# A token-mixer kernel whose phases are re-ordered as a software pipeline

## The chip, the cores and the metric

The kernel runs on one core of one Trainium2 chip. The metric is the time of one execution on the device, in microseconds (us). A profile's own length, its "span" from first to last instruction, is about 2 us shorter than that time. Engines: PE is the matmul array (TensorE), PEld its weight loads, DVE is VectorE, ACT is ScalarE, POOL is GpSimd, and SP issues most DMA transfers.

The kernel before scatters, and its slower runs have a lower granted array clock (0.903 at 284.3 us, 0.926 at 279.5 us). A run is called slow when it lies over 1.5% above the fastest.

## The reference

2048 tokens of width 448. A layer norm feeds two branches that are added at the end:

```python
x = A_x
xn = _layernorm(x, axis=-1)
return x + _A_ref(xn, A_wqkv, A_w_phi, A_wo) + _B_ref(xn, B_w1, B_w2, B_w3, B_w4)

# A: linear attention, 16 heads of 28
q, k, v = split(xn @ wqkv)
phi_q = concat(softmax(q @ w_phi), softmax(-(q @ w_phi)))    # phi_k from k alike
kv = einsum("bhsf,bhsd->bhfd", phi_k, v);  z = sum over s of phi_k
o  = (phi_q @ kv) / (phi_q @ z + 1e-6);    o @ wo

# B: mixer, then MLP
h  = gelu(layernorm(xn) @ w1)              # shifted by 1, -1, 2, -2 tokens in four channel groups
x1 = xn + shifted(h) @ w2
x1 + gelu(layernorm(x1) @ w3) @ w4         # w3 is 448x1792
```

## The kernel before

A small recorder notes each operation with what it reads and writes, then emits every engine's instructions in program order with the semaphore waits that the data needs. So the order of the Python calls is the order of each engine's queue. The work is cut into 16 tiles of 128 tokens, or 4 groups of 4 tiles. It has three stages:

```python
# front: layer norm, transposes of xn, W1
for g in range(NG):
    if g + 1 < NG:
        ln1(4 * g + 4, 4, [pool, dve])
    for i in range(4 * g, 4 * g + 4):
        xn_T(i)                       # PE transposes to banks 0, 1; ACT copies to xnT
    for m in range(NM):
        w1_chunk(g, m)                # PE; ACT applies gelu
        if g < 2:
            fold(1 - g, m)
# middle: K, V, W2 and Q of every tile, kv sums two tiles behind
for i in range(NT + 2):
    if i < NT:
        k_tile(i)
        v_tile(i)
    if i >= 2:
        kv_tile(i - 2)
    if i < NT:
        w2_tile(i)
        if i % 4 == 3:
            ln_scale(mv2, rs2, i - 3, 4)
        q_chunk(*divmod(i, 4))
kv_finish()
for i in range(4):
    g_apply(i)
    g_T(i, banks[7])
num_tile(0)
# tail: W3, W4, attention output; "fill" is dealt out between the 14 W3 chunks of a group
for g in range(NG):
    fill = []
    for j in range(4):
        i = 4 * g + j
        if i > 0:
            fill.append(lambda i=i: num_tile(i))
        if g + 1 < NG:
            fill.append(lambda i=i + 4: (g_apply(i), g_T(i, banks[7])))
        if i > 0:
            fill.append(lambda i=i - 1: o_T(i))
        if g >= 1:
            fill.append(lambda i=i - 4: fin_tile(i))
    ...                               # w3_chunk(g, fc), then the next entries of fill
```

Pieces of the tail (cut):

```python
def g_apply(i):                       # second layer norm of x1, on POOL
    ln_apply(pool, g_tok[:, i % 4, 0:D], xn[:, i, 0:D], rs2, i)
def g_T(i, b):                        # PE transposes g_tok into bank b; DVE copies to gT for W3
    ...
def num_tile(i):
    # PE: 8 matmuls of 128 columns to banks 5 and 6
    # DVE: reciprocal, three products and sums, sum, reciprocal (the "attention chain")
    R.ew(pool, "tensor_tensor", o_tok[...], q_n[...], rden[...], op=ALU.mult)   # POOL: output multiply
def o_T(i):                           # PE transposes o_tok into bank 7; DVE copies to oT
    ...
def fin_tile(i):                      # PE: 14 W4 and 4 wo matmuls of 448 columns; DVE adds; DMA out
    ...
```

Names in the profile are those of memory regions. In the tail the attention chain lives in the region `vaug`, h3T in `phik`, o_tok and oT in `hT` (in `xnT` after the change). `POOL hT<-vaug` is therefore the output multiply, and `bank<-ident,hT` the o transpose.

The softmax here doesn't subtract the row's maximum and nothing guards it: scores larger than these inputs give would overflow.

## Time and profile before

| | before |
|---|---|
| time, median of 4 runs | 279.68 us (277.62 to 284.34) |
| span of the profiled run | 282.5 us (it was a slow one, 284.2 us) |
| front, middle, tail | 0-43, 43-101.4, 101.4-282.5 us |

The first line of the profile page gives busy time, share of the span and instructions of each engine:

```profile
PE 223.5 (79%) x1277; PEld 123.7 (44%) x1289; DVE 121.2 (43%) x275; ACT 101.8 (36%) x184; POOL 93.6 (33%) x125
```

Two rows of its second part cut the span into 40 slices of 7 us; a digit is the PE's busy share, or the granted clock, in tenths:

```profile
PE   1587779999999946665866859587595959999996
...
PEclk9959999999999977989679786999977868999999
```

PE is the busiest engine, but neither row is full. The middle (slices 7 to 14) is dense at full clock. From slice 15 both rows dip again and again. The busy time in four stretches says the same in numbers; after the stretch come its length, the busy time (and instructions) of PE, PEld, DVE, ACT and POOL, the granted clock, DMA share and GB/s:

```profile
0.00:42.97 42.97, 27.80 (x194) 18.44 (x195) 18.39 (x48) 27.01 (x45) 18.28 (x48) 0.92 0.60 175
42.97:101.40 58.43, 56.66 (x321) 33.07 (x319) 43.81 (x81) 41.36 (x83) 32.12 (x28) 1.00 0.00 1
101.40:237.00 135.60, 96.49 (x514) 49.71 (x524) 43.34 (x109) 25.08 (x42) 31.43 (x38) 0.82 0.02 7
237.00:282.50 45.50, 42.51 (x252) 22.47 (x252) 15.63 (x38) 8.36 (x14) 11.81 (x12) 1.00 0.07 23
```

The long stretch from 101.4 us is the weak one: clock 0.82, and 39 us without a matmul. The waits view tells for what PE waited (total us, times, longest):

```profile
PE bank L190 <- POOL g_tok L198: 35.9, 13, 3.3
PE bank L190 <- DMA hi<-in_A_wqkv_dram: 5.7, 1, 5.7
PE bank L190 <- DVE xn L198: 2.9, 1, 2.9
```

One of the 13 waits, in the timeline (start, duration, engine, line, operation, and in brackets the idle time before it and what ended it):

```profile
130.42 1.52 DVE L198 TENSOR_TENSOR vaug<-bank,vaug 128x16 f32<-128x16 f32 x3
...
132.53 0.94 POOL L198 TENSOR_TENSOR hT<-vaug 128x448 bf16<-128x448 f32 x1 [6.15 <-DVE vaug L198]
133.45 0.72 POOL L198 TENSOR_SCALAR g_tok<-xn,rs 128x448 bf16<-128x448 bf16 x1
134.22 0.60 PE L190 MATMUL bank<-ident,g_tok 128*128 128x128 bf16 x4 [3.27 <-POOL g_tok L198]
...
134.62 1.91 PE L186 MATMUL bank<-gT,w 128*128 128x512 bf16 x4
```

POOL was idle for 6.15 us, and g_apply needs nothing that was late: it reads x1 and its statistics, ready since the middle. But it stands behind the output multiply in POOL's queue, and that waits for the attention chain on DVE. PE, which has the g transpose next, waits 3.27 us for a 0.72 us operation that could have run long before. The four 512-column matmuls after the hole take 1.91 us, at a granted clock of 0.50. The four at 126.67 us took 1.03 us, at a clock of 1.00. These two durations are what "half rate" and "full rate" mean below.

### The profile page before, as it was taken

To read this page: it belongs to the slowest core of one execution; us is meant where nothing else is said; L and a number is where in the kernel's file an instruction comes from. 1 tells how busy PE (TensorE), PEld (TensorE's weight loads), DVE (VectorE), ACT (ScalarE), POOL (GpSimd) and SP (SyncE) were. 2 spreads that over 40 slices of the span, in tenths; PEclk is the share of its full clock that TensorE was granted. 3 is DMA by queue.
4 is the path that set the end of the run, shared out by engine and by line. 5 is a ranking of instruction groups with operands and counts; after the bars stand their busy time and mean duration, and the time that the engine had idled before them with its cause. 6 is when DMAs were issued, how large, how long until landed. Compare 5 with 4: busy or idle time off the path is not lost.

```text
span 282.5 us, 3255 instructions
## 1 busy us (share of the span) xinstructions
PE 223.5 (79%) x1277; PEld 123.7 (44%) x1289; DVE 121.2 (43%) x275; ACT 101.8 (36%) x184; POOL 93.6 (33%) x125
## 2 busy tenths in 40 slices
PE   1587779999999946665866859587595959999996
PEld 0554445555555623332433424233252424555552
DVE  5377204877777754433313140441413131434311
ACT  1668768666666631323211011121111111232100
POOL 8544402464646482222031230303303030222520
PEclk9959999999999977989679786999977868999999
DMA  7997000000000000000000000000000000000000
GB/s 212 331 310 210 1 1 2 0 0 2 0 0 2 0 0 0 2 0 0 0 0 19 1 16 0 16 19 0 16 1 18 2 16 16 18 17 16 19 32 32
DMA packets 9613, 9.52 MB, mean 34 GB/s; under 512 B 1022, under 2 KB 9150, under 8 KB 9598
## 3 DMA queue, kind: packets, MB, share of 16 engines
q1 hardware_dynamic: 8176, 8.09, 9.7%
q10 hardware_dynamic: 1422, 1.23, 1.4%
q8 instruction: 10, 0.16, 0.2%
q14 instruction: 5, 0.04, 0.0%
HBM read 7.48 MB, written 1.84 MB: 33 GB/s over the span
## 4 chain that ended last, share of the span: by engine, by line
PE 67%; DVE 15%; POOL 12%; ACT 3%; issue 2%; POOLq 0%
PE bank L186 62%; DVE vaug L198 10%; PE bank L190 5%; POOL hT L198 4%; POOL g_tok L198 3%; DVE st L198 2%; ACT xnT L194 2%; POOL rs L198 1%; DVE xn L198 1%; POOL vaug L198 1%; ACT phik L194 1%; POOL kvq L198 1%; DVE mv L198 1%; POOL phik L198 1%; DVE gT L198 0%
## 5 line engine op out<-in xcount | busy, mean ns | idle before, releaser
L194 ACT ACTIVATE phik<-bank 128x512 bf16<-128x512 f32 (+1 forms) x88 | 49.2, 581 | 128.5 <-PE bank L186 128.5
L186 PE MATMUL bank<-gT,w 128*128 128x512 bf16 x212 | 63.2, 429 | 1.3 <-issue 0.4
L198 DVE TENSOR_TENSOR vaug<-bank,vaug 128x464 f32<-128x464 f32 (+2 forms) x64 | 33.3, 520 | 57.9 <-PE bank L186 56.3
L198 POOL TENSOR_TENSOR hT<-vaug 128x448 bf16<-128x448 f32 x16 | 15.1, 941 | 124.3 <-DVE vaug L198 124.3
L186 PE MATMUL bank<-w,phik 128*128 128x448 bf16 x224 | 50.3, 381 | 0.0
L198 POOL TENSOR_TENSOR phik<-phik,rks 128x896 bf16<-128x896 bf16 x16 | 27.2, 1698 | 36.0 <-DVE rks L198 35.8
L190 PE MATMUL bank<-ident,g_tok 128*128 128x128 bf16 x64 | 8.2, 270 | 37.6 <-POOL g_tok L198 35.9
L186 PEld LDWEIGHTS bank<-w,phik 128*128 128x128 bf16 x224 | 23.5, 106 | 24.3 <-issue 7.3
L186 PEld LDWEIGHTS bank<-gT,w 128*128 128x128 bf16 x224 | 22.8, 109 | 20.5 <-issue 6.9
L198 DVE TENSOR_REDUCE ksum<-phik 128x32 f32<-128x896 bf16 x16 | 17.3, 1082 | 23.3 <-ACT phik L194 23.3
L190 PEld LDWEIGHTS bank<-ident,g_tok 128*128 128x128 bf16 x64 | 4.7, 116 | 44.5 <-POOL g_tok L198 42.0
L186 PE MATMUL bank<-xnT,w 128*112 128x512 bf16 x64 | 17.6, 417 | 2.8 <-ACT xnT L194 2.8
L198 DVE COPY gT<-bank 128x512 bf16<-128x512 bf16 x16 | 6.8, 424 | 29.7 <-PE bank L190 29.7
L198 POOL TENSOR_TENSOR vaug<-xn,xtok 128x448 f32<-128x448 bf16 x16 | 16.5, 1032 | 5.7 <-DVE vaug L198 5.7
L194 ACT ACTIVATE hi<-bank 112x512 bf16<-112x512 f32 (+1 forms) x20 | 12.4, 681 | 11.6 <-PE bank L186 9.1
L186 PE MATMUL bank<-xnT,wpq 128*112 128x512 bf16 x64 | 16.5, 379 | 0.0
L186 PE MATMUL bank<-w,hT 112*128 112x448 bf16 x64 | 14.8, 352 | 0.0
L186 PE MATMUL bank<-wo,hT 128*128 128x448 bf16 x64 | 14.7, 353 | 0.0
L186 PE MATMUL bank<-wv,xnT 128*128 128x448 bf16 x64 | 14.7, 352 | 0.0
L186 PE MATMUL bank<-wpk,xnT 128*128 128x448 bf16 x64 | 14.7, 352 | 0.0
L198 DVE COPY hT<-bank 128x512 bf16<-128x512 bf16 x16 | 6.5, 408 | 13.8 <-PE bank L190 13.8
L194 ACT ACTIVATE hT<-bank 112x512 bf16<-112x512 f32 x16 | 9.6, 598 | 7.4 <-PE bank L186 7.2
(68 smaller groups left out, 250.6 us busy)
## 6 DMA issues: line engine op xcount, KB each, us to landing
out_dram<-vaug SPq DMA_DIRECT2D x16, 112.0 KB, 1.7
w<-in_B_w_dram SPq DMA_DIRECT2D x1, 1568.0 KB, 15.0
xtok<-in_A_x_dram SPq DMA_DIRECT2D x3, 448.0 KB, 8.0
w<-in_B_w_dram SPq DMA_DIRECT2D x1, 1344.0 KB, 10.8
hi<-in_A_wqkv_dram ACTq DMA_DIRECT2D x1, 672.0 KB, 4.7
xtok<-in_A_x_dram SPq DMA_DIRECT2D x4, 112.0 KB, 5.0
w<-in_B_w_dram SPq DMA_DIRECT2D x1, 392.0 KB, 9.3
w<-in_B_w_dram ACTq DMA_DIRECT2D x1, 336.0 KB, 7.4
```

What stands on the lines that cost most here:

```text
L186: self.op("PE", lambda e: e.matmul(out, lhsT, rhs, start=start, stop=stop, skip_group_check=True), [out], [lhsT, rhs])
L190: self.op("PE", lambda e: e.transpose(out, in_, ident), [out], [in_, ident])
L194: self.op("ACT", lambda e: e.activation(out, in_, func, **kw), [out], [in_] + aps)
L198: self.op(eng, lambda e: getattr(e, name)(out, *args, **kw), [out], aps)
```

## The change

The intent was a software pipeline: x is loaded first; V and W2 tiles are spread over the stages to even out the load; transposes run behind their inputs; the end of the kv sum is worked into the W3 stage. Matmuls and their shapes stay. The diff, cut to its core:

```diff
+        load_x(0, 2)
+        load_x(2, 2)
+        load_rows(wqk, A_wqkv[:, 0:896])        # was first, on ACT's queue
 ...
-            R.act(vaug[:, i, :]..., b[:, 0:D]..., ACT.Copy)
+            R.ew(dve, "tensor_copy", vaug[:, i, :]..., b[:, 0:D]...)
 ...
         for g in range(NG):                      # front
             ...
+            for i in range(4 * g + 4, min(4 * g + 8, NT)):
+                xn_T(i)                          # of the next group
+            if g < 2:
+                for i in range(4 * g, 4 * g + 4):
+                    v_tile(i)                    # 8 of the 16 V tiles
 ...
         for i in range(NT + 2):                  # middle
             if i < NT:
                 k_tile(i)
-                v_tile(i)
 ...
-                w2_tile(i)
-                if i % 4 == 3:
-                    ln_scale(mv2, rs2, i - 3, 4)
+                if i % 2 == 0:
+                    v_tile(8 + i // 2)
+                else:
+                    w2_tile(i // 2)              # W2 tiles 0 to 7
+                    ...
                 q_chunk(*divmod(i, 4))
+                if i == 9:
+                    for j in range(4):
+                        g_apply(j)
+                if i >= 12:
+                    g_T(i - 12, banks[5])
 ...
         for g in range(NG):                      # tail
             fill = []
+            if g + 1 < NG:
+                fill.append(lambda g=g: [g_apply(4 * g + 4 + j) for j in range(4)])
+            if g == 0:
+                fill.append(kv_blocks)
             for j in range(4):
                 i = 4 * g + j
-                if i > 0:
-                    fill.append(lambda i=i: num_tile(i))
+                fill.append(lambda i=i: num_tile(i))
+                if g >= 1:
+                    fill.append(lambda i=i - 4: fin_tile(i))
+                if g < 2:
+                    fill.append(lambda i=i + 8: w2_tile(i))     # W2 tiles 8 to 15
+                    ...
                 if g + 1 < NG:
-                    fill.append(lambda i=i + 4: (g_apply(i), g_T(i, banks[7])))
+                    fill.append(lambda i=i + 4: g_T(i, banks[7]))
                 if i > 0:
                     fill.append(lambda i=i - 1: o_T(i))
-                if g >= 1:
-                    fill.append(lambda i=i - 4: fin_tile(i))
```

More of the change, by code (lines that the diff above doesn't have):

```diff
@@ L244, in bass_parallel_sum__linear_kernel_hedgehog__mixer_s_mlp__prompt_kernel @@
         xn = new("xn", NT * 512).rearrange("p (t d) -> p t d", t=NT)
-        xnT = new("xnT", KC * S).rearrange("p (c s) -> p c s", c=KC)
+        xnT_r = region("xnT", KC * S * 2)
+        xnT = view(xnT_r, KC * S).rearrange("p (c s) -> p c s", c=KC)
         hT_r = region("hT", NM * HW * 2)
@@ L286, in bass_parallel_sum__linear_kernel_hedgehog__mixer_s_mlp__prompt_kernel @@
         h3T = view(phik_r, 2 * FC * 512).rearrange("p (b c f) -> p b c f", b=2, c=FC)
-        oT = view(hT_r, 2 * KC * 512).rearrange("p (b c s) -> p b c s", b=2, c=KC)
-        o_tok = view(hT_r, 4 * 512, at=2 * KC * 512 * 2).rearrange("p (b d) -> p b d", b=4)
+        oT = view(xnT_r, 2 * KC * 512).rearrange("p (b c s) -> p b c s", b=2, c=KC)
+        o_tok = view(xnT_r, 4 * 512, at=2 * KC * 512 * 2).rearrange("p (b d) -> p b d", b=4)
         o2 = 0
@@ L318, in bass_parallel_sum__linear_kernel_hedgehog__mixer_s_mlp__prompt_kernel, with load_x, load_rows @@
         dve, pool = "DVE", "POOL"
-        for i in range(4):
-            R.dma(xtok[:, i, :], x2d[128 * i:128 * i + 128, :])
-        def load_rows(dst, src, eng):
-            R.dma(dst[:, 0:3, :], src[0:384, :].rearrange("(c p) d -> p c d", p=128), eng)
-            R.dma(dst[0:64, 3, :], src[384:448, :], eng)
-        R.act(maskb[0:1, 0:1], ident[0:1, 0:1], ACT.Gelu_apprx_tanh) if False else None
-        load_rows(wqk, A_wqkv[:, 0:896], "ACT")
-        R.dma(wphi[0:DH, :].rearrange("e (h f) -> e h f", h=H), A_w_phi.rearrange("h e f -> e h f"), "ACT")
-        load_rows(w1, B_w1, "ACT")
-        for g in range(1, NG):
-            R.dma(xtok[:, 4 * g:4 * g + 4, :], x2d[512 * g:512 * g + 512, :].rearrange("(j p) d -> p j d", p=128))
-        load_rows(wv, A_wqkv[:, 896:1344], "SP")
+        def load_x(i, n):
+            R.dma(xtok[:, i:i + n, :], x2d[128 * i:128 * (i + n), :].rearrange("(j p) d -> p j d", p=128))
+        def load_rows(dst, src):
+            R.dma(dst[:, 0:3, :], src[0:384, :].rearrange("(c p) d -> p c d", p=128))
+            R.dma(dst[0:64, 3, :], src[384:448, :])
+        R.dma(wphi[0:DH, :].rearrange("e (h f) -> e h f", h=H), A_w_phi.rearrange("h e f -> e h f"), "ACT")
+        load_x(0, 2)
+        load_x(2, 2)
+        load_rows(wqk, A_wqkv[:, 0:896])
+        load_rows(w1, B_w1)
+        load_x(4, 4)
+        load_x(8, 4)
+        load_rows(wv, A_wqkv[:, 896:1344])
+        load_x(12, 4)
         R.dma(w2[0:CR, :, :], B_w2.rearrange("(m p) d -> p m d", p=CR))
-        load_rows(wo, A_wo, "SP")
-        load_rows(w3, B_w3, "SP")
+        load_rows(w3, B_w3)
+        load_rows(wo, A_wo)
         R.dma(w4[:, :, :], B_w4.rearrange("(c p) d -> p c d", p=128))
@@ L384, in ln_apply, with ln1_stats @@
             R.ew(eng, "tensor_scalar", dst, src, rst[:, i, 1:2], rst[:, i, 0:1], op0=ALU.add, op1=ALU.mult)
-        def ln1(a, n, engs):
+        def ln1_stats(a, n):
             for i in range(a, a + n):
@@ L389, in ln1, with ln1_apply @@
             ln_scale(mv, rs, a, n)
+        def ln1_apply(a, n, engs):
             for i in range(a, a + n):
@@ L429, in w1_chunk @@
             R.act(hT[0:CR, m, 2 + 512 * g:2 + 512 * g + 512], b[0:CR, :], ACT.Gelu_apprx_tanh)
+        rot = [(0, 1, 2, 3, 4, 5)]
         def rot_b():
-            return bank(0, 1, 2, 3, 4, 5)
+            return bank(*rot[0])
         def v_tile(i):
@@ L437, in v_tile @@
                 R.mm(b[:, 0:D], xnT[:, kc, 128 * i:128 * i + 128], wv[:, kc, :], kc == 0, kc == KC - 1)
-            R.act(vaug[:, i, :].rearrange("p (h e) -> p h e", e=HP)[:, :, 0:DH],
-                  b[:, 0:D].rearrange("p (h e) -> p h e", e=DH), ACT.Copy)
+            R.ew(dve, "tensor_copy", vaug[:, i, :].rearrange("p (h e) -> p h e", e=HP)[:, :, 0:DH],
+                 b[:, 0:D].rearrange("p (h e) -> p h e", e=DH))
         def k_tile(i):
@@ L457, in kv_tile, with kv_copy @@
                      i == 0 and c % 2 == 0, i == NT - 1)
-        def kv_finish():
+        def kv_copy():
             for h in range(2):
@@ L462, in kv_finish, with kv_blocks @@
                      banks[6 + h][:, 0:448].rearrange("p (c f) -> p c f", c=2))
+        def kv_blocks():
             b = banks[6]
@@ L542, in fin_tile @@
             R.dma(out2d[128 * i:128 * i + 128, :], outb[:, i % 4, :])
-        ln1(0, 2, [dve])
-        ln1(2, 2, [dve])
-        for t in range(2):
+        ln1_stats(0, 2)
+        ln1_stats(2, 2)
+        ln1_apply(0, 2, [dve])
+        ln1_apply(2, 2, [dve])
+        for t in (1, 0):
             for pair in range(2):
@@ L550, in bass_parallel_sum__linear_kernel_hedgehog__mixer_s_mlp__prompt_kernel @@
         phi_blocks()
+        for i in range(4):
+            xn_T(i)
+        ln1_stats(4, 4)
+        ln1_stats(8, 4)
+        ln1_apply(4, 4, [pool, dve])
+        rot[0] = (5, 6, 7)
         for g in range(NG):
-            if g + 1 < NG:
-                ln1(4 * g + 4, 4, [pool, dve])
-            for i in range(4 * g, 4 * g + 4):
-                xn_T(i)
             for m in range(NM):
@@ L559, in bass_parallel_sum__linear_kernel_hedgehog__mixer_s_mlp__prompt_kernel @@
                     fold(1 - g, m)
+            if g == 0:
+                ln1_stats(12, 4)
+                ln1_apply(8, 4, [pool, dve])
+            if g == 1:
+                ln1_apply(12, 4, [pool, dve])
+            for i in range(4 * g + 4, min(4 * g + 8, NT)):
+                xn_T(i)
+            if g < 2:
+                for i in range(4 * g, 4 * g + 4):
+                    v_tile(i)
+        rot[0] = (0, 1, 2, 3, 4, 5)
         for i in range(NT + 2):
@@ L566, in bass_parallel_sum__linear_kernel_hedgehog__mixer_s_mlp__prompt_kernel @@
             if i < NT:
-                w2_tile(i)
-                if i % 4 == 3:
-                    ln_scale(mv2, rs2, i - 3, 4)
-                q_chunk(*divmod(i, 4))
-        kv_finish()
+                if i % 2 == 0:
+                    v_tile(8 + i // 2)
+                else:
+                    w2_tile(i // 2)
+                    if i % 8 == 7:
+                        ln_scale(mv2, rs2, i // 2 - 3, 4)
+                q_chunk(*divmod(i, 4))
+                if i == 9:
[3 more added lines that the diff above has]
+                    g_T(i - 12, banks[5])
+                    rot[0] = (0, 1, 2, 3, 4)
+        kv_copy()
         R.ew(pool, "memset", o_tok[:, :, D:512], 0.0)
-        for i in range(4):
-            g_apply(i)
-            g_T(i, banks[7])
-        num_tile(0)
+        rot[0] = (3, 4)
         for g in range(NG):
             fill = []
+            if g + 1 < NG:
+                fill.append(lambda g=g: [g_apply(4 * g + 4 + j) for j in range(4)])
+            if g == 0:
+                fill.append(kv_blocks)
             for j in range(4):
                 i = 4 * g + j
-                if i > 0:
-                    fill.append(lambda i=i: num_tile(i))
+                fill.append(lambda i=i: num_tile(i))
[3 more added lines that the diff above has]
+                    fill.append(lambda i=i + 8: w2_tile(i))
+                    if j == 3:
+                        fill.append(lambda i=4 * g + 8: ln_scale(mv2, rs2, i, 4))
                 if g + 1 < NG:
-                    fill.append(lambda i=i + 4: (g_apply(i), g_T(i, banks[7])))
+                    fill.append(lambda i=i + 4: g_T(i, banks[7]))
                 if i > 0:
                     fill.append(lambda i=i - 1: o_T(i))
-                if g >= 1:
-                    fill.append(lambda i=i - 4: fin_tile(i))
             n = 0
```

## The prediction

> **What bounds it now.** TensorE (busy 79% of the span; the chain of waits is 62% matmul), but it runs well in only one of three stages. From busy time and granted clock by stretch:
>
> - Front (0-43 us: norms, transposes, W1): matmul busy 27.8 us. By the timeline each group of four tiles loses 1.05 us (transposes have two banks, emptied by 0.6 us ACT copies) plus 0.7 us before W1; the first W1 matmuls run at half rate.
> - Middle (43-101.4): no gaps, clock 1.00, 3.5 us per tile; 1.5 us wait for POOL at its end.
> - Tail (101.4-282.5): the waits view gives 35.9 us in 13 waits (up to 3.3 us) of the g transposes for POOL's g_tok. Each g_apply stands in POOL's queue behind the output multiply (0.94 us), which waits for the DVE attention chain (2.3 us). After such holes the clock falls: four 512-column matmuls start over 1.71 us instead of 0.86; mean clock 0.82 in 101.4-237. The last group, without g transposes (237-264), runs dense at 1.00.
>
> [...] after the 3.27 us gap before 134.2 the clock is 0.50, while the front's ~1 us gaps leave 1.00.
>
> **Work.** Matmul counts stay. From trace rates (0.215 us per 512 columns, 0.19 per 448, about 0.056 per 128) all matmul work is about 195 us at full clock (estimate). So about 85 us of 279 is holes and slow clock, some 60 of it in the tail.
>
> **What the change does.**
> 1. Four g_applys go to the head of each group's POOL work, a group early: the 35.9 us of waits and the half-rate stretches after them go. Main effect.
> 2. Eight V tiles (6.1 us of PE) fill the front's holes; eight W2 tiles (6.1 us) move to the tail.
> 3. V copies (0.57 us) move from ACT to DVE. Middle per two tiles: PE 5.5 us, DVE about 4.9 plus overheads, ACT 4.6. Nearly balanced: small stalls.
>
> **New stages (estimates from trace durations).**
> - Front: wqk queues behind x, so PE starts about 1 us later, but POOL's rs (8.6 us) and ACT's wT copies gate W1 anyway. Two-bank waits stay. End about 42, with 8 V tiles done.
> - Middle: 16x2.76 + 0.9 = 45 us of PE. The chain k matmul, exp, reduce, reciprocal, POOL, kv takes 4.7 us against 5.5 available; four g_applys at tile 9 (2.9 us of POOL) and ln_scale (1.4 us) overrun that; the last kv waits about 2 us. About 50 us.
> - Tail: first group DVE-bound: per tile 2.3 chain + 1.4 W2 add and statistics + 0.83 copies = 4.5 us, against 4.8 PE, and the o transpose shares bank 7 with the g transpose, whose copy queues behind the statistics: 1-2 us stall per tile, about 24 us. Groups 2-4 about 35, 31, 29; last four outputs 14; end 3. About 135.
>
> Sum: **227 us, 80% range 216 to 240**. Chances: faster by over 2% 0.98, within 0.015, slower 0.005.
>
> **What would show each step.** PE wait for g_tok below 3 us; tail clock at least 0.97; PE busy falls from 223 to 200-208; middle waits for POOL phik, largest near tile 9 and at the end; tail waits of transposes for the copy of gT, mostly in the first two groups; front about 42 us; ACT busy down 9 us, DVE up 9.
>
> **What would make it wrong.** If 1-2 us stalls in the first tail group trip the clock: 235-245. If DVE delays the kv chain every tile: +5-10. If the front's V tiles wait for DVE copies behind the norm statistics: +3. If bank-7 stalls are mostly hidden: 217.

A rule for idle gaps that no trace or run of this case shows is cut from the prediction, with the remark that the trace agrees with it; the measured gaps stay. Its sum: 42 + 50 + 135 = 227 us.

## The result

| | before | after |
|---|---|---|
| time, median of 4 runs | 279.68 us | 233.80 us (233.19 to 234.70) |
| ratio, 95% interval | | 0.838 (0.832 to 0.844) |
| span of the profiled run | 282.5 us | 231.3 us |
| front / middle / tail | 43.0 / 58.4 / 181.1 us | 46.5 / 48.8 / 136.0 us |

Ratios are the mean time of one kernel's fast runs over that of the kernel before in the same rounds, so not quite the ratio of the medians. The stages do not hold the same work: before, the tail is counted from the end of the kv sum, 7 us ahead of the first W3 matmul (108.4 us); after, it starts with the first W3 matmul (95.3 us), and eight W2 tiles have moved into it.

The same views of the changed kernel. Busy times:

```profile
PE 204.6 (88%) x1289; PEld 115.9 (50%) x1289; DVE 128.1 (55%) x291; ACT 94.8 (41%) x168; POOL 93.1 (40%) x125
```

The 40 slices, now of 5.8 us:

```profile
PE   0568989798999999696999889989999999999995
...
PEclk9988999999999999998899999999999999999999
```

The stretches:

```profile
0.00:46.46 46.46, 32.51 (x225) 20.89 (x226) 22.03 (x56) 26.99 (x45) 17.97 (x48) 0.96 0.59 162
46.46:95.29 48.83, 45.60 (x273) 27.61 (x272) 37.83 (x68) 34.39 (x67) 31.52 (x25) 1.00 0.00 1
95.29:231.30 136.01, 126.52 (x794) 67.39 (x792) 68.20 (x167) 33.43 (x56) 43.61 (x53) 0.98 0.04 14
```

The waits of PE:

```profile
PE bank L190 <- DMA hi<-in_A_wqkv_dram: 8.3, 2, 8.2
PE bank L190 <- DVE gT L198: 5.6, 6, 2.1
PE bank L186 <- POOL phik L198: 3.2, 3, 1.7
PE bank L190 <- ACT xnT L194: 2.9, 3, 1.1
PE bank L186 <- ACT xnT L194: 1.5, 2, 0.8
```

The 35.9 us of waits for g_tok are gone, and the clock of the tail is 0.98. PE's busy time fell by 19 us although it does the same matmuls: far fewer of them run at half rate (the W3 matmuls of 512 columns take 386 ns each on average instead of 429). The front, however, became 3.5 us longer, with 8 V tiles more in it (6.1 us of PE). Its PE timeline shows how few of them went into holes. The first W1 matmuls and the step from the x transposes to W1 of group 1, before:

```profile
15.70 1.95 PE L186 MATMUL bank<-xnT,w 128*112 128x512 bf16 x4 [0.75 <-ACT xnT L194]
...
23.90 0.87 PE L190 MATMUL bank<-ident,xn 128*128 128x128 bf16 x8 [1.05 <-POOL rs L198]
25.46 1.07 PE L186 MATMUL bank<-xnT,w 128*112 128x512 bf16 x4 [0.69 <-ACT xnT L194]
```

and after:

```profile
15.63 1.95 PE L186 MATMUL bank<-xnT,w 128*112 128x512 bf16 x4 [0.69 <-ACT xnT L194]
...
23.21 0.87 PE L190 MATMUL bank<-ident,xn 128*128 128x128 bf16 x8 [1.05 <-POOL rs L198]
23.92 3.19 PE L186 MATMUL bank<-wv,xnT 128*128 128x448 bf16 x16
26.95 1.03 PE L186 MATMUL bank<-xnT,w 128*112 128x512 bf16 x4
```

W1 starts at the same time, though PE's first instruction comes 2.5 us later (8.18 against 5.65 us). In group 1 the step takes 3.74 us instead of 1.56, so of 3.03 us of V tiles only 0.85 went into a hole. Group 2 is alike (0.93). That makes 1.8 of 6.1 us; another 0.6 us came from the W1 chunks of group 0, which happened to run at half rate for a shorter time (the second and third took 1.64 and 1.03 us instead of 1.91 and 1.24).

A new wait is the one for the copy of gT. The longest, in the timeline of the first tail group:

```profile
96.77 2.80 POOL L198 TENSOR_SCALAR g_tok<-xn,rs 128x448 bf16<-128x448 bf16 x4
...
104.96 0.39 PE L190 MATMUL bank<-ident,g_tok 128*128 128x128 bf16 x4
...
105.63 0.56 DVE L198 TENSOR_TENSOR xn<-bank,xn 128x448 bf16<-128x448 f32 x1
...
106.23 0.63 DVE L198 BATCH_NORM_STATS2 st<-xn 128x6 f32<-128x448 bf16 x1
106.89 0.18 DVE L198 BATCH_NORM_AGGREGATE mv<-st 128x2 f32<-128x6 f32 x1
106.99 0.39 DVE L198 COPY gT<-bank 128x512 bf16<-128x512 bf16 x1
...
107.44 0.40 PE L190 MATMUL bank<-ident,xnT 128*128 128x128 bf16 x4 [2.09 <-DVE gT L198]
...
107.67 1.85 PE L186 MATMUL bank<-gT,w 128*128 128x512 bf16 x4
```

The four g_applys (first line) are done at 99.57 us, 5.4 us before the transpose at 104.96. The o transpose at 107.44 uses the same bank 7, which is free only when DVE has copied gT out, and that copy stands behind the W2 add and statistics. After this hole of 2.09 us four 512-column matmuls took 1.85 us at a clock of 0.52: half rate once more.

### The profile page after: what moved, and what is told of

It reads as the page before. It is cut to its first block, busy times and chain, and to the rows that moved or that the text cites. A ratio compares the mean times of both kernels' runs of the same rounds, so it can differ in the third digit from the quotient of the medians.

```text
span 231.3 us, 3260 instructions
## 1 busy us (share of the span) xinstructions
PE 204.6 (88%) x1289; PEld 115.9 (50%) x1289; DVE 128.1 (55%) x291; ACT 94.8 (41%) x168; POOL 93.1 (40%) x125
## 4 chain that ended last, share of the span: by engine, by line
PE 62%; DVE 20%; POOL 7%; ACT 5%; DMA 3%; issue 2%; SPq 1%; DVEq 0%
PE bank L186 57%; DVE vaug L198 8%; PE bank L190 5%; DVE st L198 5%; POOL phik L198 3%; DMA hi<-in_A_wqkv_dram 3%; DVE xn L198 2%; DVE mv L198 1%; DVE ksum L198 1%; DVE gT L198 1%; POOL vaug L198 1%; POOL xnT L198 1%; POOL g_tok L198 1%; ACT phik L194 1%; ACT hi L194 1%
## 5 line engine op out<-in xcount | busy, mean ns | idle before, releaser
L186 PE MATMUL bank<-gT,w 128*128 128x512 bf16 x224 | 57.8, 386 | 0.0
L186 PE MATMUL bank<-w,phik 128*128 128x448 bf16 x224 | 45.0, 352 | 0.0
L198 POOL TENSOR_TENSOR xnT<-vaug 128x448 bf16<-128x448 f32 x16 | 15.1, 941 | 73.8 <-DVE vaug L198 73.8
L186 PEld LDWEIGHTS bank<-w,phik 128*128 128x128 bf16 x224 | 21.8, 98 | 20.7
L186 PEld LDWEIGHTS bank<-gT,w 128*128 128x128 bf16 x224 | 20.8, 99 | 18.3 <-issue 1.1
L186 PE MATMUL bank<-wo,xnT 128*128 128x448 bf16 x64 | 14.7, 352 | 0.0
L198 DVE CAST vaug<-bank 128x448 bf16<-128x448 f32 x16 | 9.5, 593 | 8.6 <-PE bank L186 7.8
L198 DVE RECIPROCAL vaug<-bank 128x16 f32<-128x16 f32 x16 | 4.1, 257 | 15.2 <-PE bank L186 15.2
L190 PE MATMUL bank<-ident,xnT 128*128 128x128 bf16 x64 | 6.3, 221 | 6.3 <-DVE gT L198 5.6
L186 PE MATMUL bank<-phik,vaug 128*128 128x224 bf16 x64 | 8.8, 259 | 3.2 <-POOL phik L198 3.2
```

Source lines behind the costliest of these rows:

```text
L186: self.op("PE", lambda e: e.matmul(out, lhsT, rhs, start=start, stop=stop, skip_group_check=True), [out], [lhsT, rhs])
L190: self.op("PE", lambda e: e.transpose(out, in_, ident), [out], [in_, ident])
L198: self.op(eng, lambda e: getattr(e, name)(out, *args, **kw), [out], aps)
```

## The experiments

Twelve kernels ran, all gave the right result, and all their runs were fast but one of e6 (229.6 us, left out of its ratio). "Before" is that kernel on the same chip, in the same job. By the record's own classing e8, e2, e6, e5 and e12 are "faster" than it and the others "unclear"; but all intervals end at 0.963 or below.

| run | what it is | us | before | ratio (95%) |
|---|---|---|---|---|
| e1_hoist_only | before + hoist | 240.8 | 281.5 | 0.858 (0.852-0.864) |
| e7_fin_first | before + lag | 246.0 | 281.5 | 0.876 (0.870-0.882) |
| e8_both | before + hoist + lag | 234.2 | 280.4 | 0.838 (0.833-0.843) |
| e3_warm_holes | before + dummy matmuls in the holes | 267.6 | 281.5 | 0.954 (0.945-0.963) |
| e2_unhoist | after - hoist | 245.1 | 280.4 | 0.875 (0.869-0.882) |
| e4_no_spread | after - spread of V and W2 | 231.0 | 281.5 | 0.822 (0.816-0.828) |
| e6_gT_first | after, g transpose ahead of W2 | 228.7 | 280.4 | 0.815 (0.808-0.823) |
| e5_wqk_first | after, wqk loaded first | 232.4 | 280.4 | 0.833 (0.826-0.839) |
| e9_early_rs | e4 + wqk first + POOL memsets later | 228.3 | 280.0 | 0.821 (0.811-0.830) |
| e10_best | e9 + front re-ordered | 230.5 | 280.0 | 0.828 (0.818-0.838) |
| e11_warm_start | e10 + dummy matmuls at the start | 229.4 | 280.0 | 0.824 (0.817-0.832) |
| e12_combined | e9 + selected parts of e10 | 226.6 | 279.8 | 0.815 (0.809-0.820) |

The theory: the gain is the waits for g_tok and the half-rate matmuls behind them, and two small moves in the tail's order take them away. The rival: the spread of V and W2, the loads and the late kv finish carry a good part.

### One part alone: the hoist

```diff
             fill = []
+            if g + 1 < NG:
+                fill.append(lambda g=g: [g_apply(4 * g + 4 + j) for j in range(4)])
 ...
-                    fill.append(lambda i=i + 4: (g_apply(i), g_T(i, banks[7])))
+                    fill.append(lambda i=i + 4: g_T(i, banks[7]))
```

> The kernel before with one part of the change: the four g_apply calls of the next group stand at the head of each group's POOL work. Theory A (the gain is the 35.9 us of waits for g_tok plus the half-rate matmuls after them; the rest of the re-ordering adds little): PE waits for g_tok below 3 us from 107 us on, mean clock of the tail 0.97 or more, time 231 to 240 us. Theory B (the moved V and W2 tiles, the x-first loads and the late kv finish each carry a part): 245 us or more.

Measured 240.8 us, just above theory A's range and well below theory B's. The clock from its first W3 matmul on (108.8 us) is 0.99. Its waits of PE:

```profile
PE bank L190 <- DVE gT L198: 10.1, 12, 1.6
...
PE bank L190 <- POOL g_tok L198: 0.9, 2, 0.5
```

The waits for g_tok went from 35.9 to 0.9 us. But 10.1 us of a wait appeared that had been 1.7 us: with the g transposes no longer late, the o transpose now follows while the gT copy is still queued on DVE. Three lines of order are worth 40.7 us.

### The other part alone: the lag

```diff
                     fill.append(lambda i=i: num_tile(i))
+                if g >= 1:
+                    fill.append(lambda i=i - 4: fin_tile(i))
                 if g + 1 < NG:
                     fill.append(lambda i=i + 4: (g_apply(i), g_T(i, banks[7])))
 ...
-                if g >= 1:
-                    fill.append(lambda i=i - 4: fin_tile(i))
```

> The kernel before with another part alone: in each slot the output tile of the group before is put ahead of the g transpose, so that 3.4 us of matmuls cover the POOL chain; g_apply stays where it was. There is no such tile in group 0. If the lag alone is enough where it exists: waits for g_tok fall from 35.9 to about 13 us (4 times 3.3 in group 0), time about 243 us (237 to 250). If only the place in POOL's queue counts: 270 us or more.

Measured 246.0 us, as expected. Its waits for g_tok:

```profile
PE bank L190 <- POOL g_tok L198: 9.8, 5, 3.3
```

The four over 1 us are in group 0 (1.19 to 3.27 us). Where an output tile stands between, its 3.4 us of matmuls cover the chain through DVE and POOL.

### Both, and nothing else

> The kernel before with the two parts of the earlier runs together: g_apply at the head of the group, and the output tile ahead of the g transpose. Alone they gave 240.8 and 246.0 us from 281.5. Theory A (both remove the same waits, so they overlap, and what is left are the transposes' waits for the gT copy, 10.1 us with the first part alone, which the second spreads apart): 233 to 238 us, that is within 2% of the changed kernel without any of its other moves. Theory B (the other moves of the change add a further 3% or more): 241 us or more.

The edit is the two diffs above together. Measured 234.2 us, ratio 0.838 (0.833 to 0.843). The changed kernel has 0.838 (0.832 to 0.844). So these two moves give the whole gain, within the measurement, and everything else in the change nets out to nothing (the spread, taken out below, shows that the rest has parts of both signs). Its waits show how they complement each other:

```profile
PE bank L190 <- DVE gT L198: 3.5, 6, 0.7
...
PE bank L190 <- POOL g_tok L198: 1.3, 2, 1.0
```

### The hoist taken out of the changed kernel

```diff
-            if g + 1 < NG:
-                fill.append(lambda g=g: [g_apply(4 * g + 4 + j) for j in range(4)])
 ...
-                    fill.append(lambda i=i + 4: g_T(i, banks[7]))
+                    fill.append(lambda i=i + 4: (g_apply(i), g_T(i, banks[7])))
```

> The changed kernel with g_apply put back directly ahead of each g transpose, in POOL's queue behind the output multiply of the slot; all else as changed. If the hoist is needed there: waits for g_tok in group 0 of 2 us per tile (W2 and W3 cover part of the 4 us chain), none in groups 1 and 2 where an output tile stands between; 10 to 14 us more than 233.8, so 242 to 250 us. If the lag of the transposes alone is enough in the changed kernel: within 2% (229 to 238 us).

Measured 245.1 us, with 10.9 us of waits for g_tok in 5 waits, four of them in group 0 and one of 2.3 us in group 2. That last one (until 164.93 us) has another cause, by the order of the code: in POOL's queue g_apply stands there behind the rs of the W2 tiles that the spread had moved. At the same place in the changed kernel POOL waited 3.16 us for their statistics and then made rs from 154.57 to 156.17 us. The lag covers groups 1 and 2; the hoist is needed for group 0, as in the kernel before.

### Waits or clock: the holes filled with dummy matmuls

```diff
+        def dummy(n):
+            for _ in range(n):
+                R.mm(banks[7][:, :], ident[:, :], w3[:, 0, 0:512], True, True)
 ...
-                    fill.append(lambda i=i + 4: (g_apply(i), g_T(i, banks[7])))
+                    fill.append(lambda i=i + 4: (g_apply(i), dummy(8), g_T(i, banks[7])))
```

> The kernel before with 8 dummy matmuls of 512 columns (1.7 us at full clock) ahead of each g transpose of groups 0 to 2, into the bank that the transpose then overwrites: the waits stay, the array stays busy in them. It separates the slow clock from the waits. Theory A1 (the half rate after the holes is worth some 15 to 20 us of its own): clock of the tail 0.97 or more, time 260 to 266 us. Rival A2 (slow matmuls hide behind the same waits and cost nothing): 275 us or more although the clock is up.

Measured 267.6 us, 13.9 us less than before; that lies between the two expectations and nearer to A1's. Its waits, and the place that was shown above for the kernel before:

```profile
PE bank L190 <- POOL g_tok L198: 15.6, 12, 1.5
```

```profile
129.43 1.89 PE L186 MATMUL bank<-w,ident 128*128 128x512 bf16 x8
132.86 0.40 PE L190 MATMUL bank<-ident,g_tok 128*128 128x128 bf16 x4 [1.54 <-POOL g_tok L198]
133.09 1.03 PE L186 MATMUL bank<-gT,w 128*128 128x512 bf16 x4
```

The stretch from its first W3 matmul on:

```profile
107.94:266.00 158.06, 139.44 (x842) 71.47 (x840) 55.51 (x140) 33.44 (x56) 39.47 (x44) 1.00 0.04 12
```

The waits did not get shorter. The 15.6 us that are left and 12 times 1.72 us of dummy work (estimate: 8 times 0.215 us each) make 36 us, the 35.9 us of before. But the clock is up to 1.00, and the matmuls after them take 1.03 us per four instead of 1.91. So the slow clock alone cost about 14 us by the medians, and rival A2 is out. The two profiled executions differ by 17.0 us (282.5 against 265.5), but the one of the kernel before was a slow one, with a clock of 0.903; so what the half rate costs differs from execution to execution. The rest of the gain, 267.6 down to the 234 of both moves, is 33 us. It fits the waits that went: those for g_tok and gT together fell from 37.6 to 4.8 us (e8).

### The spread of V and W2 undone

```diff
-            if g < 2:
-                for i in range(4 * g, 4 * g + 4):
-                    v_tile(i)
 ...
                 k_tile(i)
+                v_tile(i)
 ...
-                if i % 2 == 0:
-                    v_tile(8 + i // 2)
-                else:
-                    w2_tile(i // 2)
-                    ...
+                w2_tile(i)
+                if i % 4 == 3:
+                    ln_scale(mv2, rs2, i - 3, 4)
 ...
-                if g < 2:
-                    fill.append(lambda i=i + 8: w2_tile(i))
-                    ...
```

The V copy went back to ACT.

> The changed kernel with all V and W2 tiles back in the middle, one each per tile as before, and the V copy back on ACT; everything else as changed. Theory A (spreading is not where the gain is; the array is the bound in all stages, and W2 in the tail costs DVE waits): front about 40.4 us, middle about 59, tail about 125; time 224 to 231 us, so faster than the changed kernel's 233.8. Theory B (spreading pays, as intended): 237 us or more.

Measured 231.0 us, at the upper edge of theory A's range, and against theory B. Its ratio, 0.822, lies clear of the changed kernel's 0.838 (the two ran in different jobs; the difference is 1.2% by the times and 1.9% by the ratios). The stretches:

```profile
0.00:44.74 44.74, 28.48 (x193) 18.70 (x194) 17.94 (x48) 27.02 (x45) 18.07 (x48) 0.92 0.62 168
44.74:103.21 58.47, 57.40 (x337) 34.06 (x336) 44.63 (x84) 41.02 (x83) 34.58 (x31) 1.00 0.00 1
103.21:229.20 125.99, 118.63 (x762) 63.28 (x760) 57.67 (x143) 33.81 (x57) 40.73 (x47) 1.00 0.05 15
```

The middle is 9.6 us longer, the tail 10.0 us shorter, the front 1.7 us shorter. In this trace PE started a microsecond later (9.1 us) and part of group 1's W1 ran at half rate (its second chunk took 1.92 us), which is why the front was 44.7 and not the expected 40.4. Spreading moved 12 us of matmuls out of a stage that was dense at full clock, into a front whose holes took 1.8 us of them and a tail where W2's add and statistics (1.37 us per tile) delay the copies on DVE. In the middle and the tail of the changed kernel PE is busy for 93% of the time, so its work there can be moved but hardly hidden. A second pair agrees: e9, which is without the spread, ran at 228.3 us, and e5, which has it, at 232.4; both load wqk first, but e9 also has its memsets later. Which of the three parts that this run takes back (V tiles, W2 tiles, the V copy) costs how much is not separated, except that the next run shows the W2 statistics at work. Against e8, which has only the hoist and the lag (234.2 us), this run is some 3 us faster: that is what the other moves are worth without the spread, as far as runs of two jobs can be compared, and the spread takes it back.

### The g transpose ahead of W2

```diff
+                if g + 1 < NG:
+                    fill.append(lambda i=i + 4: g_T(i, banks[7]))
                 if g < 2:
                     fill.append(lambda i=i + 8: w2_tile(i))
                     ...
-                if g + 1 < NG:
-                    fill.append(lambda i=i + 4: g_T(i, banks[7]))
```

> The changed kernel with each g transpose of the tail put ahead of the W2 tile of its slot, so that its DVE copy no longer queues behind the W2 statistics and frees bank 7 for the o transpose earlier. Theory A (the waits for the gT copy, 5.6 us in all with the longest of 2.1 us, come from that queue, and the half-rate stretch at 107 to 111 us follows from the longest): these waits below 2 us, no clock drop near 107 us, 226 to 230 us. Rival (DVE is the bound of group 0, so the wait only moves): within 1% of 233.8.

Measured 228.7 us (226.2 to 229.6). The waits for gT fell from 5.6 to this:

```profile
PE bank L190 <- DVE gT L198: 1.2, 2, 0.7
```

The tail's clock is 1.00 and its length 128.9 us instead of 136.0. The 7.1 us are more than the 4.4 us of waits that went; no stretch near 107 us runs at half rate any more (four W3 matmuls at 106.39 and at 109.11 us take 1.03 us; the clock from 98.13 to 110 us is 1.00). Theory A holds. The whole gained less than the tail, because the front of this execution, with the same front code, ended at 49.27 us instead of 46.46: more of its W1 ran at half rate (the last group took 5.35 us instead of 3.66). So the length of one and the same front differs by 2.8 us between these two executions.

### The order of the loads

```diff
+        load_rows(wqk, A_wqkv[:, 0:896], "ACT")
 ...
-        load_rows(wqk, A_wqkv[:, 0:896])
```

> The changed kernel with the wqk load issued first and from ACT's queue, as in the kernel before. The array then starts at 5.5 to 6 us instead of 8.2. By the prediction POOL's rs (8.6 us) and ACT's wT copies gate W1, so W1 starts at most 1 us earlier: time down by 0 to 1 us. Rival (the x-first order is what delayed the front, which ended at 46.5 us instead of the 42 predicted): W1 starts 2 us or more earlier, time 231.5 us or less.

Measured 232.4 us. Its ratio, 0.833 (0.826 to 0.839), is not clear of the changed kernel's. The first W1 matmuls started at 14.36 us instead of 15.63: 1.3 us earlier, between the two expectations (at most 1, and 2 or more). But the front ended at 46.37 instead of 46.46 us: nothing was won. The first twelve W1 matmuls of this run (timeline):

```profile
14.36 1.95 PE L186 MATMUL bank<-xnT,w 128*112 128x512 bf16 x4 [0.69 <-ACT xnT L194]
...
16.48 1.91 PE L186 MATMUL bank<-xnT,w 128*112 128x512 bf16 x4
...
18.56 1.79 PE L186 MATMUL bank<-xnT,w 128*112 128x512 bf16 x4
```

Starting earlier only meant that more of W1 ran at half rate: the four W1 chunks with their folds took 7.1 us (14.36 to 21.45) against 5.9 us (15.63 to 21.55) in the changed kernel. The 1.2 us in the tail's length (134.8 against 136.0) explain the difference of the two profiled runs; it is not an effect of the load order that this run can show.

### What gates W1

In e9 the late POOL memsets are put behind the first two scale computations, on top of e4 and of wqk first:

```diff
-        R.ew(pool, "memset", vp[:, :, DH:HP], 0.0)      # and kvq, hT, g_tok
 ...
         ln1_stats(2, 2)
+        late_memsets()
         ln1_apply(0, 2, [dve])
```

> The changed kernel without the spread of V and W2 (which ran at 231.0), with wqk loaded first, and POOL's memsets of vaug, kvq, hT and g_tok moved behind the first two scale computations, so that rs is ready near 6.5 us instead of 8.6. If rs gates the start of W1: W1 starts 1.5 us or more earlier than the 14.4 us of the run with wqk first. If wqk's arrival and ACT's four wT copies (3.8 us) gate it, as the prediction's second reason says: W1 still starts at 14 to 14.5 us. Time 228 to 231 us either way, front end 39 to 42 us.

Measured 228.3 us; W1 started at 14.29 us, although the first rs was now ready at 7.4 us (9.9 us in e5). So rs is not what W1 waits for. What comes before W1 is the arrival of wqk (its second piece let PE go on at 7.3 us), the weight transposes (to 10.6 us) and their four ACT copies (to 11.9 us), behind which ACT copies xnT. The front ended at 42.2 us, just above what was expected.

### Two attempts at the front, and the combination

In e10 the query weight's transposes go between the W1 chunks, the x transposes of groups 2 and 3 stand singly between the chunks of the group before, some copies move to DVE, and the start of W3 fills the wait before the last kv tile:

```diff
-        for t in (1, 0):
-            for pair in range(2):
-                weight_T(t, pair)
+        weight_T(1, 0)
+        weight_T(1, 1)
 ...
+                if g == 0 and m % 2 == 1:
+                    weight_T(0, m // 2)
+                if 1 <= g < 3:
+                    xn_T(4 * g + 4 + m)
 ...
+                if i == NT + 1:
+                    w3_chunk(0, 0)
+                    w3_chunk(0, 1)
                 kv_tile(i - 2)
```

> The same with the front re-ordered: only the two key weight transposes ahead of the x transposes, the two query ones between W1 chunks; x transposes of groups 2 and 3 one by one between the W1 chunks of the group before, their copies and those of the folded query weight on DVE; g_apply and g transposes of group 0 four tiles earlier; two W3 chunks of group 0 between the last two kv tiles. The array's waits of the front for the copies of xnT (4 to 6 us) and the last wait for phik (1.1 to 1.7 us) should go: W1 starts near 11 to 12 us, front ends at 34 to 37, time 220 to 225 us. If ACT or DVE in the front bounds it instead: front end 38 or later, 226 us or more.

Measured 230.5 us: it failed, as its second expectation has it. W1 started at 13.18 us, but the front ended at 44.96. The line that shows why:

```profile
31.06 0.40 PE L190 MATMUL bank<-ident,xn 128*128 128x128 bf16 x4 [2.69 <-DVE xnT L198]
```

The copies that were moved to DVE stand there behind the norm work of group 3, in which DVE itself waited 1.71 us for POOL's rs (until 29.12 us). From 33.65 us on W1 of group 2 then ran at half rate (1.96 us per four). The last wait for phik did go.

> The run before this one with 36 dummy matmuls of 128 columns (3.9 us at half rate) while the array waits for wqk. In all kernels the weight transposes start at half rate (103 ns per 128 columns) and the first W1 matmuls too (0.43 us per 512 columns). If the half rate comes from the idle time before: both run at full rate, 2 to 3 us less than the run before. If the gaps between the transposes bring the half rate back anyway: no change (within 1 us).

Measured 229.4 us (229.2 to 229.6) against e10's 230.5 (229.0 to 231.8): the ranges overlap, so it is unclear. The trace is plainer. With 36 dummy matmuls at the start the weight transposes ran at full rate (13 in 0.93 us instead of 1.64), but the first W1 chunk at 13.08 us took 1.96 us again: the gaps of 0.7 to 0.8 us between the x transposes had come between.

> The run with the early rs (228.3 us) plus, from the failed re-ordering of the front, only the parts that its trace did not show to hurt: x transposes of groups 2 and 3 one by one between W1 chunks, odd copies of those on DVE (norm work of group 3 queued ahead of them); g_apply and g transposes of group 0 four tiles earlier; two W3 chunks between the last two kv tiles; and in the tail the order g transpose, attention tile, output tile, o transpose, so that neither copy of bank 7 queues behind the attention chain. Expected: the last wait for phik (1.1 us) and the waits for gT (3.2 us) go, of the front's waits for xnT about 3 of 6 us: 221 to 225 us. If the waits only move between engines: 227 us or more.

The last kernel keeps from e10 the single x transposes of groups 2 and 3 (with group 3's norm work ahead of the copies), the early g transposes and the W3 chunks before the last kv tile; its tail has the order g transpose, attention tile, output tile, o transpose. Measured 226.6 us (224.7 to 227.4): between the two expectations, and the lowest median. The front ended at 38.1 us and no wait for phik is left. The tail, 126.6 us, is no shorter than e9's 125.9: the waits of the o transposes for gT became waits, mostly of the g transposes, for the copy of o (3.0 us in all, 5 times) and one of 1.4 us for g_tok. Its ratio, 0.815 (0.809 to 0.820), is clear of the changed kernel's 0.838, but not of e6's 0.815 (0.808 to 0.823), which needs two moved lines.

## Why the prediction was right

The prediction was 227 us with 216 to 240 as the range; 233.8 us was measured. The mechanism and the direction held, and the size was 6.8 us off.

- **Main effect: right, shown.** Waits for g_tok below 3 us were predicted and none is left; clock of the tail at least 0.97, it is 0.98; PE busy 200 to 208 us, it is 204.6. Runs e1, e7 and e8 show that the hoist and the lag are the cause, e3 splits their effect into about 14 us of clock and 33 us of waits. The prediction named only the hoist; the lag alone does almost as much, and the two overlap: in the changed kernel the hoist is worth only 11 us (e2). So the credit was wrongly given, though the waits went as said. The number did not suffer: the tail was summed up group by group in the new order, which holds both.
- **Tail 135 us: measured 136.0.** By groups, between the first W3 chunks in the timeline (95.29, 119.63, 155.07, 185.34 us; the outputs from 214.66): 24.3, 35.4, 30.3 and 29.3 us, then 13.6 us of outputs and 3.0 us of end; predicted were 24, 35, 31, 29, 14 and 3. The stall of the o transpose behind the gT copy was there as named, and e6 shows its cause.
- **Middle 50 us: measured 48.8.** Small waits for POOL phik (0.8, 0.7 and 1.7 us), largest at the end, as said; near tile 9 the overrun was milder than feared.
- **Front "about 42, with 8 V tiles done": wrong, measured 46.5.** This is the term of the sum that was mis-sized. The step that failed is "Eight V tiles (6.1 us of PE) fill the front's holes". They took the place of the waits before W1 of groups 1 and 2, 1.8 us in all, and the other 4.3 us of them made the front longer: the two-bank waits of 1.05 us stayed, as the prediction itself says, and the first W1 matmuls ran at half rate as before (1.95 us per four in both). Its own figures did not allow more: 1.05 and 0.7 us of holes in each of two groups are 3.5 us, so 43.0 + 6.1 - 3.5 would have been 45.6 us and not 42 (estimate). PE's start was mis-sized too (8.2 us, 2.5 us later than before, not "about 1 us"), but it cost nothing: W1 started at 15.63 us, 15.70 before, so the reason "gate W1 anyway" held for the time, if not for rs (e9). What the front's half rate adds varies: in e5 an earlier start gave an equally late end, and e6's front, with the same code, took 49.3 us.
- **The sum was a span.** The prediction added up a span and called it the time, which is 2 us longer. Against the profiled run's 233.3 us the terms add up: front +4.5, middle -1.2, tail +1.0, the span's 2.0; the median lies another 0.5 us higher.
- **"Eight W2 tiles move to the tail": counted, but its sign not.** The prediction listed the spread among what the change does and did not ask whether it pays. Run e4 shows that it costs: without it 231.0 us.
- **ACT down and DVE up by 9 us: too much.** They moved by 7.0 and 6.9 us.

What remains open is after which holes the clock falls (see the last section), and what of the front's half rate could be saved.

## What to carry to other kernels

An operation whose inputs are long ready should not stand in an in-order queue behind one that waits (here a 0.72 us g_apply stood behind an output multiply for which POOL waited 6.15 us); look for an engine that is idle for microseconds just before a short operation on which the bottleneck waits. Then look at what the bottleneck can do in the meantime: here the hoist and the lag each gave about 35 to 41 of the 46 us, and the same two edits alone, without the rest of the re-ordering, gave all of it. Moving work from a dense stage into stages with holes did not pay here: the holes took 1.8 of the 6.1 us of V tiles, and the helpers of the moved W2 tiles (1.37 us each on DVE) delayed the copies of gT; so test that part by itself.

## What the traces show of the clock

- The length of a gap of PE does not by itself tell what follows. In the changed kernel a gap of 2.09 us, with four transposes next to it on each side, was followed by half rate (four 512-column matmuls in 1.85 us), while in e7 one of 3.27 us was not (1.03 us). In the kernel before a gap of 3.27 us was followed by half rate at 134.6 us (four in 1.91 us) and by full rate at 193.0 us (three in 0.81 us). Why, no run here tests.
- The transposes of 128x128 run at the higher rate too. The g transposes take 219 ns each (median) in the changed kernel and 288 ns in the kernel before; there four of them took 0.60 us at 134.22 us, where the clock was 0.50, and 0.40 us at 126.43 us. With dummy matmuls ahead of them (e11), 13 weight transposes took 0.93 us instead of the 1.64 of e10.
- The mean clock of a profile misled in e5: it is told as 1.000, though the first W1 chunk took 1.95 us instead of 1.03. The durations of equal matmuls are the safer reading there.
- What the half rate costs the kernel before can be estimated from its clock. Cut into windows of 0.3 us, its stretch from 101.4 to 237 us is at 0.50 for 45.3 us, at 1.00 for 84.9 us and in between for 5.4 us; that amounts to 48 us of half rate. At half rate four W3 matmuls start over 1.71 us instead of 0.86, so about half of the 48 us, 24 us, is lost (estimate). Taking the half rate away (e3) won 13.9 us by the medians, and 17.0 us between the profiled executions, which is what the 24 us must be held against. Some 5 of the 48 us are in windows in which PE ran nothing; the rest of the difference is not explained by any run here.
